# Three order strings of a one-core convolution-and-gate kernel are laid anew

## The chip, the core and the metric

The kernel runs on one core of a Trainium2 chip. The core has five instruction streams that run side by side: PE (TensorE, matrix products), DVE (VectorE), ACT (ScalarE), POOL (GpSimd) and SP (SyncE, which here only starts transfers). Each stream takes its instructions in the order of the program and waits, by semaphores, for what it needs from others. Matrix products land in PSUM; an *eviction* copies or casts a PSUM tile to SBUF, and is done by DVE or by ACT. Transfers between SBUF and DRAM are started from SP, ACT or POOL.

The metric is the device time of one execution in microseconds (us). Of the kernel before there are three timed runs and one profiled execution.

## The reference

For one sequence of 2048 positions and 512 channels the forward pass is

```python
xn = _layernorm(x)
# S4 part: a diagonal state space model with 128 modes a channel, as a long convolution
P = exp(dt * A * l)                       # l = 0 .. 2047
K = einsum("dn,dnl,dn->dl", C, P, dt * B).real
s = irfft(rfft(pad(xn)) * rfft(pad(K)))[:L] + xn * Dskip
# gate: two matrix products, 512 -> 1792 -> 512
g = silu(silu(xn @ w1) @ w2)
out = x + s * g
```

The kernel must give `out` and, for a given `grad_out`, the gradients of u, A (real, imaginary), B (real, imaginary), C (real, imaginary), log_dt, Dskip, w1 and w2: twelve outputs in bf16.

## The kernel before

The work is cut into stages. Stage 1 makes the powers of the modes, runs the gate's forward pass and stores most of its results in DRAM. Stage 2, the *table stage*, makes the filter K for four blocks of 128 channels. For a block b = 1 to 3 the kernel loads the compact tables X and XYc (`open_tables`, `open_y`), ACT copies XYc into CY (`copy_tables`, L869 and L870), and DVE multiplies the tables out in five steps (`chunk_tables`, L884 to L905: products over X, over CY, and three more over X). PE then makes K from X and CY (`chunk_K`, tile ps_k, evicted to Kout), and it also transposes the finished rows of X (`gen_xt`, L1012, tile pt_xt, evicted to XT and stored as XTd for the backward pass). Beside this the layernormed input xn and the gradient tile DS go through the first half of a Fourier transform (`spectrum`: tiles ps_f, evicted to FA; a *turn* of FA, that is two 32 x 32 block transposes on DVE at L162; ps_s, evicted to FX), and w2 is transposed (`gen_w2t`, tile pt_w, evicted to w2o). `store_K` (L956) writes K to Kud in DRAM.

Stage 3 reads K back in another layout (`load_K`, K_b, L976 to L983, started from SP, ACT and POOL), transforms it (FA, FX again), multiplies the spectra with those of xn and DS (XP loads on POOL, `cplx_mul` L125 and L126), transforms back (tile ps_i, evicted to FZ, turned at L162; then ps_v), and writes the convolution outputs DXC and S_s (`evs`, L104). Stage 5 runs the backward pass of the state space part (`Slabs.steps`: Gbd L1624, ps_V to Vb, T L1649), of the gate (`all_dh`, `all_dx`, ps_w to KXW, dhT L1740), the weight gradients (`grads`, L1901, from the tile dhc, which is loaded at L1870) and the output (`Out0`, L1450 to L1463: for each of eight pieces of the sequence, loads of zS, zg and zx from SP, two DVE products, and a store that is started one piece later; a piece has two buffers a name).

What sets the order of all this are strings written out by hand. `play` (L109) takes a string, and for each letter lets one generator go one step on; the letter names the generator (`t` one group of transposes, `g` one table step, `u` a step of the spectrum of xn, `f` that of DS, and so on). If the letter is a capital, the PSUM evictions of that step are done by DVE (`k.by_dve`, L77 in `ev`, L104 in `evs`), otherwise by ACT. All instructions are then in the order in which the steps ran, each on its engine. Steps that only start transfers (`o`, the loads of X; `k` in stage 3, those of XP) are letters too.

```python
def ev(k, out, in_):
    (k.nc.vector.tensor_copy if k.by_dve else k.nc.scalar.copy)(out=out, in_=in_)

    for ch in score:
        kk.by_dve = ch.isupper()
        next(parts[ch.lower()], None)
```

SCORE_1 orders stage 1, SCORE_2 the table stage, SCORE_3 the leftovers of the table stage, the filter transform and the convolutions, and SCORE_5 the backward pass in three parts. What a string does not reach is drained behind it.

Of the kernel before, what the change touches and what calls it, by code (L numbers as in the profile page):

```python
# [30 lines left out]

SCORE_1 = "pppppggppgppppppppgpggpppppppgppppgppgppgppppppppppgppppppppgppgpppgppppgpgpppppMgppppgppppppppgpppppgppmpgpmpppgpgppmpmpgpppgpgmppppgppmpMmgpgpmmpmggGmttgmtmGtgmtgggGgggGGg"
SCORE_2 = (
    "uguuuuuutUtuwKttttgTckggktukggttttotututuTtgtg",
    "tcutgutgkTkgkkoutt",
    "uutuutuuuuKgugwctUktuw",
    "uuwgtugkgttuTtktWuKkKkt",
)
SCORE_3 = (
    "TTtTUU",  # L40
    "FFFFffTuffTqfkqqqfffqFfkUffFffTfDfuTfUfDffkdkd",
    "FaddaafadkfdddFaknddFdafaffFbDsvvvavdsndngbFagnsbdbkgggadkadidaidadDpDbiabjpdsjbaaadxipbxvvxvxxvexsizjBgziepgegggzjtzxxtizeszjzXzibtzjbyybfebpbybsbpbxxjpssxxpyxlxxesxzglzczqxsjesysezzyzlsczYsCzsYZCsCCCC",
)
SCORE_5 = (
    "uywuuWWLWhywl",
    "yLhWYluYYyLwlwwLuhylwulHlllHwYllwYyYuhLwlyLlyWhwwyhwywLHwllYWwLWLlwHWylyWLlWhwwllyLoholoolhlLlYoLooYyllYlHllxlxxLlLhxlxlxxll",
    "zxzhxHHfxHxhfxhfhxxxxHxHxHxhhtftttfhxxxfHxzmxxHxtftttffzmtMtftxmxtxmtzfffMxfMftftmftxzMMxzffzmrtzrmzrr",
)


# [1903 lines left out]
```

## Time and profile before

| what | value |
|---|---|
| median of 3 runs | 688.61 us (688.0 to 692.97) |
| the profiled execution | 691.96 us, span 690.2 us |
| granted PE clock over the span | 0.943 of full speed |
| busy, share of the span: PE, DVE, ACT, POOL | 84%, 84%, 64%, 14% |
| DRAM read and written | 76.81 and 67.65 MB, 209 GB/s over the span |

The page gives one execution. Busy time is the time in which an engine runs an instruction, so a span of 690.2 us with PE at 84% has some 110 us in which PE waits for another engine, a transfer, or a buffer. Times of a trace's rows are counted from the start of the span. The table stage begins near 150.8 us; K is stored near 241.4 us; the convolutions end near 408 us.

### The profile page before, as it was taken

The page shows a single profiled execution, that of the slowest core. Times are in us where ns is not written, and L with a number is a line of the kernel's source. Part 1 is how long each engine was busy: PE and PEld are TensorE (multiplying, and loading weights), DVE is VectorE, ACT ScalarE, POOL GpSimd, SP SyncE. Part 2 cuts the span into 40 slices and gives each one's busy share as a digit, 9 for nine tenths or more (in the row PEclk, how much of TensorE's full clock was granted, in tenths as well). Part 3 has the DMA queues.
Part 4 walks back from the last instruction along what each step waited for, and adds up shares of the span by engine and source line. Part 5 has one row for each costly group of instructions (what it writes and reads, how often), then busy time and mean ns, then how long its engine had stood idle before and what let it go on. Part 6 is the DMA issues. An engine that isn't in the chain of part 4 may idle for free. (4 is left out here: it accounts for less than half of the span.)

```text
span 690.2 us, 14325 instructions
## 1 busy us (share of the span) xinstructions
PE 576.4 (84%) x5668; PEld 339.3 (49%) x5668; DVE 578.2 (84%) x954; ACT 444.3 (64%) x537; POOL 95.4 (14%) x170
## 2 busy tenths in 40 slices
PE   2977978877666868889988778899987989999896
PEld 1433433346545756566765544354544535454452
DVE  6898999789977467998999879977888978888656
ACT  4899999968779646999799615454164344443221
POOL 1120000201001232111232142121011000000000
PEclk9999999988988889999999989899998999999998
DMA  8664758778896699946477688979979559677786
GB/s 253 229 226 173 271 198 274 263 256 241 234 267 204 202 243 307 302 161 196 130 239 205 150 244 225 245 208 185 225 198 229 152 171 250 185 235 236 275 260 214
DMA packets 173622, 154.58 MB, mean 224 GB/s; under 512 B 70574, under 2 KB 141750, under 8 KB 173556
## 3 DMA queue, kind: packets, MB, share of 16 engines
q1 hardware_dynamic: 157428, 112.70, 57.3%
q0 software_dynamic: 11920, 38.08, 17.3%
q10 hardware_dynamic: 4208, 2.89, 1.5%
q8 instruction: 44, 0.72, 0.4%
q14 instruction: 22, 0.18, 0.1%
HBM read 76.81 MB, written 67.65 MB: 209 GB/s over the span
## 5 line engine op out<-in xcount | busy, mean ns | idle before, releaser
L723 PE MATMUL ps_h<-XNT,W 128*128 128x512 bf16 x224 | 58.2, 409 | 21.3 <-ACT hs L77 14.6
L1739 PE MATMUL ps_da<-DOT,W2T 128*128 128x512 bf16 x224 | 57.1, 401 | 0.7 <-DVE Vb L77 0.5
L696 PE MATMUL ps_o<-W,aT 128*128 128x512 bf16 x224 | 55.3, 396 | 1.4 <-ACT aT L725 1.4
L1801 PE MATMUL ps_dx<-KXW,dhT 128*128 128x512 bf16 x224 | 53.4, 386 | 0.0
L1568 PE MATMUL ps_w<-DO_all,KXW 128*128 128x512 bf16 x224 | 51.9, 379 | 0.7 <-DVE KXW L77 0.4
L1901 PE MATMUL ps_w<-dhc,xn 128*128 128x448 bf16 x256 | 49.7, 352 | 2.0 <-DVE o10b L77 1.9
L77 ACT CAST FA<-ps_f 128x1024 bf16<-128x1024 f32 x43 | 42.4, 1046 | 11.0 <-DMA K_b<-Kud 7.0
L77 ACT CAST FZ<-ps_i 128x1024 bf16<-128x1024 f32 x46 | 45.8, 1047 | 3.9 <-PE ps_i L187 3.8
L723 PEld LDWEIGHTS <-W 128*128 128x128 bf16 x224 | 22.7, 102 | 51.2 <-issue 26.7
L1810 ACT ACTIVATE dxn<-dxn,c,rstd 128x512 f32<-128x512 f32 x16 | 13.0, 814 | 47.4 <-DVE c L1809 47.4
L173 PE MATMUL ps_s<-FA,Wf 128*64 128x256 bf16 x384 | 35.0, 316 | 8.0 <-DVE FA L162 5.3
L1740 DVE TENSOR_TENSOR dhT<-ps_da,sd 128x1024 bf16<-128x1024 f32 x28 | 34.1, 1220 | 8.6 <-ACT sd L213 4.5
L696 PEld LDWEIGHTS <-aT 128*128 128x128 bf16 x224 | 22.9, 103 | 31.8 <-issue 6.5
L1901 PEld LDWEIGHTS <-xn 128*128 128x128 bf16 x256 | 25.0, 98 | 26.0 <-issue 2.5
L77 ACT CAST Vb<-ps_V 128x1024 bf16<-128x1024 f32 x22 | 22.0, 1014 | 24.5 <-PE ps_V L1637 18.2
L1739 PEld LDWEIGHTS <-W2T 128*128 128x128 bf16 x224 | 22.3, 103 | 28.9 <-issue 8.1
L187 PEld LDWEIGHTS <-Vi 64*128 64x128 bf16 x576 | 28.3, 98 | 15.6 <-issue 4.5
L1360 PE MATMUL ps_v<-FZ,TI 128*128 128x256 bf16 x192 | 26.4, 290 | 11.2 <-DVE FZ L162 10.3
L187 PE MATMUL ps_i<-XP,Vi 64*128 64x256 bf16 x256 | 32.0, 288 | 2.8 <-ACT KXW L77 2.4
L1801 PEld LDWEIGHTS <-dhT 128*128 128x128 bf16 x224 | 21.4, 99 | 24.6 <-issue 2.8
L725 ACT ACTIVATE aT<-ps_h 128x1024 bf16<-128x1024 f32 x28 | 31.2, 1115 | 3.3 <-PE ps_h L723 3.2
L1568 PEld LDWEIGHTS <-KXW 128*128 128x128 bf16 x224 | 20.8, 98 | 25.0 <-issue 3.3
(311 smaller groups left out, 1454.2 us busy)
## 6 DMA issues: line engine op xcount, KB each, us to landing
XTd<-XT SPq DMA_DIRECT2D x20, 512.0 KB
XP<-UXd POOLq DMA_DIRECT2D x16, 512.0 KB, 5.1
XTl<-XTd SPq DMA_DIRECT2D x31, 256.0 KB
hTd<-hs SPq DMA_DIRECT2D x28, 256.0 KB
aTd<-aT SPq DMA_DIRECT2D x28, 256.0 KB
dhc<-dhd SPq DMA_DIRECT2D x16, 448.0 KB
XYd<-XYg SPq DMA_DIRECT2D x25, 256.0 KB
hsb<-hTd SPq DMA_DIRECT2D x18, 256.0 KB
```

The costliest lines, as they stand in the source:

```text
L77: (k.nc.vector.tensor_copy if k.by_dve else k.nc.scalar.copy)(out=out, in_=in_)
L173: nc.tensor.matmul(out=ps[64 * h:64 * h + 64, c, j], lhsT=k.Wf[:, c, 0:64], rhs=A[:, 2 * (v + j) + h], start=True, stop=True)
L187: nc.tensor.matmul(out=ps[:, h, j], lhsT=Vc[z], rhs=y[z, c, v % 4 + j, :], start=(n == 0), stop=(n == len(Y) - 1))
L696: nc.tensor.matmul(out=pso[:], lhsT=aT[:, ft, tt * P:(tt + 1) * P], rhs=W2[:, ft, :], start=(ft == 0), stop=(ft == FT - 1))
L723: nc.tensor.matmul(out=ps[:, j], lhsT=W1[:, dk, ft * P:(ft + 1) * P], rhs=XNT[:, dk], start=(dk == 0), stop=(dk == DK - 1))
L725: nc.scalar.activation(out=aT[:, f0:f0 + 2, :], in_=ps[:], func=ACT.Silu)
L1360: k.nc.tensor.matmul(out=ps[:, j], lhsT=k.TI[:, t0 + j, c, :], rhs=Z[:, 2 * (t0 + j) + c], start=(c == 0), stop=(c == 1))
L1568: nc.tensor.matmul(out=ps[:], lhsT=A[:, t, :], rhs=k.DO[:, t, :], start=(t == 0), stop=(t == T - 1))
L1739: nc.tensor.matmul(out=ps[:, j], lhsT=self.W2T[:, ft // 2, dk, j * P:(j + 1) * P], rhs=self.DOT[tc_][:, dk], start=(dk == 0), stop=(dk == ...
L1740: nc.vector.tensor_tensor(out=self.dhT[:, f0:f0 + 2, :], in0=ps[:], in1=sd[:], op=ALU.mult)
L1801: nc.tensor.matmul(out=psx[:], lhsT=dhT[:, ft, t % 4 * P:(t % 4 + 1) * P], rhs=self.W1T[:, ft, :], start=(ft == 0), stop=(ft == FT - 1))
L1901: nc.tensor.matmul(out=ps[:], lhsT=k.xn[:, t, dk * P:(dk + 1) * P], rhs=ch[i][:, t, :], start=(t == 0), stop=(t == T - 1))
```

## The change

Only the three strings SCORE_2, SCORE_3 and SCORE_5 are written anew. SCORE_1, every function and the set of matrix products stay. The strings were laid with a planner in which transfers of different queues are taken to share the rate of the memory. Each step occurs as often as before; what changes is where it stands and which engine does its evictions. The first part of SCORE_2 and the last of SCORE_5:

```diff
 SCORE_2 = (
-    "uguuuuuutUtuwKttttgTckggktukggttttotututuTtgtg",
+    "uuuuugutTTUKtTWuKuTtkTtgcTgtkgggttuuuoguttutcTkT",
...
 SCORE_5 = (
...
-    "zxzhxHHfxHxhfxhfhxxxxHxHxHxhhtftttfhxxxfHxzmxxHxtftttffzmtMtftxmxtxmtzfffMxfMftftmftxzMMxzffzmrtzrmzrr",
+    "zxHxzhzHxHxhxhfHxfxfxxxHhfxxHhttHftthxxxhfxzmxHxfxttxfxmxfttxftMzxtttxmttffffMtMmtzMffzzffmrtfmrzmrzmr",
```

What it moves on the engines is seen in their instructions. On DVE, where the first table step of block 1 (L901 with 128x1792) begins in the table stage, the row before it is the last small step of block 0. The order before:

```order
L905 TENSOR_TENSOR X<-m_1686 128x2x128
L77 CAST FA<-ps_f 128x4x64x4
L162 STREAM_TRANSPOSE FA<-FA 128x32x2x32 x2
L901 TENSOR_TENSOR m_1879<-X 128x1792
L903 TENSOR_TENSOR m_1880<-X 128x7x128 x2
L904 TENSOR_TENSOR X<-m_1879 128x7x128
L905 TENSOR_TENSOR X<-m_1880 128x7x128
```

And the same place in the new order:

```order
L905 TENSOR_TENSOR X<-m_1710 128x2x128
L77 COPY XT<-pt_xt 128x1024 x2
L77 CAST FA<-ps_f 128x4x64x4
L77 COPY XT<-pt_xt 128x1024
L77 COPY w2o<-pt_w_1848 128x1024
L77 CAST Kout<-ps_k 128x41x16
L162 STREAM_TRANSPOSE FA<-FA 128x32x2x32 x2
L77 COPY XT<-pt_xt 128x1024 x2
L901 TENSOR_TENSOR m_2043<-X 128x1792
L903 TENSOR_TENSOR m_2044<-X 128x7x128 x2
```

Seven evictions that ACT did, or that DVE did later, now stand on DVE before the first step of block 1.

On DVE at the border of the convolutions and the backward pass, the last turn and the five last evictions of DXC, before:

```order
L162 STREAM_TRANSPOSE FZ<-FZ 128x32x2x32 x2
L104 TENSOR_SCALAR DXC<-ps_v 128x4x256 x5
L77 CAST KXW<-ps_w_5948 128x512
L1624 TENSOR_TENSOR Gbd<-Gt,MK 128x16x32 x2
L77 CAST Vb<-ps_V 128x4x256
L1624 TENSOR_TENSOR Gbd<-Gt,MK 128x16x32 x2
L77 CAST KXW<-ps_w_5970 128x512
L1718 COPY DOT<-pt_do 128x1024
```

And now:

```order
L77 CAST FZ<-ps_i 128x2x2x64x4
L162 STREAM_TRANSPOSE FZ<-FZ 128x32x2x32 x2
L104 TENSOR_SCALAR DXC<-ps_v 128x4x256 x5
L1624 TENSOR_TENSOR Gbd<-Gt,MK 128x16x32 x2
L77 CAST Vb<-ps_V 128x4x256
L1624 TENSOR_TENSOR Gbd<-Gt,MK 128x16x32 x2
L77 CAST KXW<-ps_w_5950 128x512
L1718 COPY DOT<-pt_do 128x1024
```

The first KXW cast, which stood ahead of Gbd, is gone from there, and the cast that is left stands behind the second Gbd.

On SP at the end of the program, where `Out0` stores a piece of the output (L91) and loads zS, zg and zx of the next (L1450), before:

```order
L1450 DMA zg<-gd 128x1024
L1450 DMA zx<-in_A_u_dram 128x1024
L1517 DMA out_dram<-ob_9034 128x4x128
L91 DMA out_dram<-zS 128x1024
L1450 DMA zS<-Sd 128x1024
L1450 DMA zg<-gd 128x1024
L1450 DMA zx<-in_A_u_dram 128x1024
L1787 DMA out_dram<-O_9022 128x512
L1787 DMA out_dram<-O_9079 128x512
L91 DMA out_dram<-zS 128x1024 x2
```

And now, from the loads of the last piece but one on:

```order
L1450 DMA zx<-in_A_u_dram 128x1024
L91 DMA out_dram<-zS 128x1024
L1450 DMA zS<-Sd 128x1024
L1450 DMA zg<-gd 128x1024
L1450 DMA zx<-in_A_u_dram 128x1024
L1517 DMA out_dram<-ob_8997 128x4x128
L1517 DMA out_dram<-ob_9003 128x4x128
L1787 DMA out_dram<-O_8840 128x512
L1787 DMA out_dram<-O_9035 128x512
L91 DMA out_dram<-zS 128x1024 x2
```

Between the last loads and the stores of the last two pieces there were two other output stores; now there are four. One step of `Out0` more stands near the start of the string's last part.

More of the change, by code (lines that the diff above doesn't have):

```diff
@@ L33 @@
 SCORE_2 = (
-    "uguuuuuutUtuwKttttgTckggktukggttttotututuTtgtg",
-    "tcutgutgkTkgkkoutt",
-    "uutuutuuuuKgugwctUktuw",
-    "uuwgtugkgttuTtktWuKkKkt",
+    "uuuuugutTTUKtTWuKuTtkTtgcTgtkgggttuuuoguttutcTkT",
+    "Tgt",
+    "TgktggkkotTguuuuuuuuwtuuuttUKkkWkttctwggugtuuutugtuWuTtTKkK",
+    "kT",
 )
 SCORE_3 = (
-    "TTtTUU",
-    "FFFFffTuffTqfkqqqfffqFfkUffFffTfDfuTfUfDffkdkd",
-    "FaddaafadkfdddFaknddFdafaffFbDsvvvavdsndngbFagnsbdbkgggadkadidaidadDpDbiabjpdsjbaaadxipbxvvxvxxvexsizjBgziepgegggzjtzxxtizeszjzXzibtzjbyybfebpbybsbpbxxjpssxxpyxlxxesxzglzczqxsjesysezzyzlsczYsCzsYZCsCCCC",
+    "TTu",
+    "FkFFFFFfqfutqqqftfffqTFkfFnfDfkUfffffTDfffddFuddU",
+    "aaafdkAffdddnaknDsdFadffafaFiDbbvBvvbvkddnsgksbadagasbgagFkdddGddaDqpijDbdpabaaadxxxiexvjepvtvvizzjgzBxjptgszxesgiggietxxzizizjzjbbbXfzyygbpsbbbeycbpxsyxzxxppsxsxxxelxcsjjzescszyselzsyzsyszlYzZZCCCCC",
 )
 SCORE_5 = (
-    "uywuuWWLWhywl",
-    "yLhWYluYYyLwlwwLuhylwulHlllHwYllwYyYuhLwlyLlyWhwwyhwywLHwllYWwLWLlwHWylyWLlWhwwllyLoholoolhlLlYoLooYyllYlHllxlxxLlLhxlxlxxll",
-    "zxzhxHHfxHxhfxhfhxxxxHxHxHxhhtftttfhxxxfHxzmxxHxtftttffzmtMtftxmxtxmtzfffMxfMftftmftxzMMxzffzmrtzrmzrr",
+    "uyuuwuuLlWWhywwWYuYYLwhllhwwllLlYHHWwlhLuyWll",
+    "LyhwWYLYwlHYlylWLllwwywwllywylWHllywlwYllYWyLHwwwylylloYHoLoYlhoLHoolollhlYLxlhLxLLxxxllxxll",
+    "zxHxzhzHxHxhxhfHxfxfxxxHhfxxHhttHftthxxxhfxzmxHxfxttxfxmxfttxftMzxtttxmttffffMtMmtzMffzzffmrtfmrzmrzmr",
 )
```

## The prediction

> **What bounds the kernel now.** I first read the table of windows, since the three order strings that change belong to stages that lie one behind the other. Columns: span of the window, busy time of PE, weight loads, VectorE (DVE), ScalarE (ACT) and GpSimd (POOL), granted clock, DMA share, GB/s.
>
> ```profile
> core 0: us, PE busy (x) PEld busy (x) DVE busy (x) ACT busy (x) POOL busy (x), PEclk, DMA share, GB/s
> 0.00:150.80 150.80, 117.45 (x571) 54.02 (x572) 130.87 (x320) 132.87 (x177) 16.98 (x33) 0.95 0.72 241
> 150.80:246.00 95.20, 69.14 (x1569) 55.27 (x1570) 75.34 (x127) 73.70 (x83) 12.37 (x22) 0.86 0.75 226
> 246.00:277.50 31.50, 22.83 (x257) 18.25 (x256) 21.04 (x27) 18.15 (x20) 10.16 (x19) 0.95 1.05 286
> 277.50:407.00 129.50, 109.44 (x1293) 80.33 (x1292) 121.20 (x108) 104.82 (x113) 32.70 (x54) 0.95 0.67 198
> 407.00:520.00 113.00, 103.73 (x954) 53.20 (x953) 97.27 (x143) 51.10 (x57) 18.69 (x34) 0.96 0.91 219
> 560.00:690.20 130.20, 121.04 (x682) 60.88 (x680) 96.45 (x177) 45.38 (x71) 0.56 (x1) 0.97 0.77 236
> ```
>
> The first window is laid by SCORE_1, which stays, so its 150.8 us stay. The table stage (to 246) is bound by no engine: PE, DVE and ACT are each busy 69 to 75 of 95.2 us, and wait for one another. In 246 to 277.5 the filter K comes back from DRAM, and the DMA share stands at its ceiling. From 277.5 to 407 DVE is busy 121.2 of 129.5, with ACT close behind. After 407 PE carries it: 103.7 of 113, then 121.0 of 130.2. So an order can win most in the table stage, where 95.2 − 75.3 = 19.9 us of DVE are idle, and little elsewhere.
>
> Next I read the waits and the DVE's own rows there, to see what the idle time is.
>
> ```profile
> DVE XT L77 <- PE pt_xt L1012: 16.0, 3, 9.7
> ACT FA L77 <- DMA K_b<-Kud: 7.0, 1, 7.0
> ACT Y L1035 <- DMA XYy<-XYd: 17.6, 1, 17.6
> ```
> ```profile
> 160.97 1.22 DVE L77 CAST FA<-ps_f 128x1024 bf16<-128x1024 f32 x1 [1.30 <-PE ps_f L148]
> 162.30 4.52 DVE L162 STREAM_TRANSPOSE FA<-FA 128x2048 f32<-128x2048 f32 x2
> 166.75 1.04 DVE L901 TENSOR_TENSOR m<-X 128x1792 bf16<-128x1792 bf16 x1
> ...
> 215.76 4.51 DVE L162 STREAM_TRANSPOSE FA<-FA 128x2048 f32<-128x2048 f32 x2 [4.17 <-ACT FA L77]
> ...
> 230.74 0.28 DVE L905 TENSOR_TENSOR X<-m 128x256 bf16<-128x256 bf16 x1
> ...
> 242.23 1.29 DVE L77 COPY XT<-pt_xt 128x1024 bf16<-128x1024 bf16 x2 [9.66 <-PE pt_xt L1012]
> 243.69 0.69 DVE L77 COPY XT<-pt_xt 128x1024 bf16<-128x1024 bf16 x1 [0.17 <-issue]
> 244.33 2.36 DVE L77 CAST FX<-ps_s 128x1024 bf16<-128x1024 f32 x2
> ```
> ```profile
> 241.39 2.34 SPq L956 DMA_DIRECT2D Kud<-Kout  x2
> ```
>
> The DVE multiplies the tables of three blocks one after the other, and the last product of block 3 ends at 230.74 + 0.28 = 231.0. Then the PE makes the last part of K, and at 241.39 SP stores it. **This chain, table products to K stored to K loaded, is the path of the table stage.** That ACT then waits 7.0 us for K_b says the same from the other end.
>
> **The change part by part.** No instruction is added or removed. Twelve PSUM evictions go from ACT to DVE over all stages behind SCORE_1 (in net), and each engine's order is new. Prices by these groups (columns: count, busy us, mean ns, idle before):
>
> ```profile
> L77 DVE COPY XT<-pt_xt 128x1024 bf16<-128x1024 bf16 x10 | 6.8, 686 | 16.2 <-PE pt_xt L1012 16.0 <-issue 0.2
> L77 DVE CAST FA<-ps_f 128x1024 bf16<-128x1024 f32 x5 | 5.8, 1215 | 1.3 <-PE ps_f L148 1.3
> L77 ACT COPY XT<-pt_xt 128x1024 bf16<-128x1024 bf16 x30 | 30.1, 1051 | 2.7 <-PE pt_xt L1012 1.1 <-DMA X<-XYd 0.8 <-ACT Kout L77 0.7
> L77 ACT CAST FA<-ps_f 128x1024 bf16<-128x1024 f32 x28 | 27.3, 1056 | 9.6 <-DMA K_b<-Kud 7.0 <-PE ps_f L148 2.5
> L77 ACT CAST Kout<-ps_k 128x656 bf16<-128x656 f32 x8 | 5.7, 712 | 8.9 <-PE ps_k L938 8.9
> ```
>
> *Term 1, the table chain.* Before, between the FA cast and the first product of block 1 the DVE has only a turn. Now seven evictions stand there beside the cast: five XT copies, one w2o copy and one Kout cast. Back to back an XT copy takes 1.29 / 2 = 0.65, so 5 × 0.65 = 3.3; w2o is as large, 0.7; the Kout cast is not in the trace on DVE and lies between ACT's 0.71 and the 1.22 of the larger cast; I take 0.8, being nearer in size to the first. Sum 4.8. These copies must also wait for their transposes. Such a wait costs between 0 and the mean 16.0 / 3 = 5.3 of the row above; I take 3, because the transposes follow each other closely in the order. So block 1 begins some 8 us later. One thing gives back: before, the turn at 215.76 stood 4.17 us for ACT's casts, and a DVE that comes later finds them done, so about 8 − 4 = 4 us are left at the end of block 3. Of this a further half microsecond goes as some K work of earlier blocks is now further ahead. **+3.5 at the store of K**; its ends are −10.1 (second rival) and +18.5 (first rival).
>
> *Term 2, behind the table chain up to 407.* Between K's store and the filter transform the order leaves out two FX casts (2.36) and one XT copy (0.65) on DVE: −3.0. Up to the last turn of that transform DVE then takes over about three casts (six FA in a row instead of four are two of them), 3 × 1.22 = +3.6; those can fall into the 31.5 − 21.0 = 10.5 us that DVE idles in 246 to 277.5. In the convolutions one cast goes back to ACT in net, −1.1 where DVE is busy 121.2 of 129.5. The ends are −3.0 − 1.1 = −4.1 and −3.0 + 3.6 − 1.1 = −0.5. As DVE waits there for K's loads and not for itself, I take a value nearer to the second, **−1.8**.
>
> [...]
>
> *Term 3, the start of the backward pass.* Before, DVE comes out of the five last convolution evictions and stands 2.10 us for a KXW cast whose matmuls have just begun; behind it wait the two products Gbd that need nothing of it.
>
> ```profile
> 406.03 2.35 DVE L104 TENSOR_SCALAR DXC<-ps_v 128x1024 bf16<-128x1024 f32 x2 [0.48 <-PE ps_v L1360]
> 410.48 0.69 DVE L77 CAST KXW<-ps_w 128x512 bf16<-128x512 f32 x1 [2.10 <-PE ps_w L1568]
> 411.09 1.28 DVE L1624 TENSOR_TENSOR Gbd<-Gt,MK 128x512 bf16<-128x512 bf16 x2
> ```
>
> Now Gbd stands first, and what it feeds (ps_V, then Vb) starts as much earlier: **−2.0** of the 2.10; it is 0 if the Gt loads are the next to be late. ACT's 17.6 us for XYy stay; ACT has little to do at that point in either order.
>
> *Term 4, the tail.*
>
> ```profile
> 663.40 0.86 SPq L91 DMA_DIRECT2D out_dram<-zS  x1
> 668.78 0.32 SPq L1450 DMA_DIRECT2D zS<-Sd  x1
> ...
> 680.78 0.33 SPq L1450 DMA_DIRECT2D zS<-Sd  x1
> ...
> 684.74 0.69 DVE L1462 TENSOR_TENSOR zS<-zS,zg 128x1024 bf16<-128x1024 bf16 x1 [2.85 <-DMA zg<-gd]
> ...
> 687.97 0.29 SPq L1084 DMA_DIRECT2D out_dram<-row  x1
> ```
> ```profile
> 664.69 18.32 PE L1901 MATMUL ps_w<-dhc,xn 128*128 128x448 bf16 x96
> ```
>
> The last PE work of size ends at 664.69 + 18.32 = 683.0, the last output row leaves at 687.97. What lies between is SP's chain of Out0: store a piece, wait until it landed, load the next into its buffer, multiply, and so on, (680.78 − 668.78) / 2 = 6.0 us a round. DVE's last reduction for the row stands behind the last such product and its 2.85 us of waiting. In the new order one more of these pieces is done before the tail, and the x steps end earlier, so that the PE has nothing but its last groups. The wait goes, and PE's end is next: an o10b eviction and its store. **−2.5** (0 to −4: the row can't leave before PE's last group, 683.0 and its eviction).
>
> *Sum:* 3.5 − 1.8 − 2.0 − 2.5 = −2.8. The profiled execution took 691.96 (span 690.2), so it becomes 689.2. The median of the three runs is 688.61, 3.35 below the profiled one; on that footing 688.61 − 2.8 = **685.8**. Terms 1 and 4 have the widest ends.
>
> **The rivals.**
>
> *First, slower: the PE is held behind the transposes.* PE, like DVE, takes its instructions in order. If a group of transposes that now stands early waits for the whole table of its block, PE holds everything behind it, spectra and chunks alike, for the delay of each block: 8 + 7 + 3.5 = +18.5 at the store of K (block 2 being late by 8 less the 0.5 to 1.1 us it waited for X). The decision lies where the first of those groups reads its X rows: from the third product on, the rows of a group are the last to be ready. For it speaks that DVE has already waited 9.66 us in one piece for transposes. Against it: before, transposes of block 1 ran at 173.95, while the table's last products ran at 183.76, so a group needs only its rows.
>
> ```profile
> 173.95 1.63 PE L1012 MATMUL pt_xt<-ident_bfloat,X 128*128 128x128 bf16 x26
> ...
> 183.76 0.28 DVE L905 TENSOR_TENSOR X<-m 128x256 bf16<-128x256 bf16 x1
> ```
>
> Time: 688.61 + 18.5 − 1.8 − 2.0 − 2.5 = 700.8.
>
> *Second, faster: ACT paces the table stage.* ACT loses there seven XT copies (7 × 1.05), two w2o (2 × 1.02, their size being XT's) and a Kout cast (0.71): 10.1 us. If it was ACT's evictions that made PE wait for PSUM, the stage shortens by up to that: 688.61 − 10.1 − 1.8 − 2.0 − 2.5 = 672.2. For it: DVE copies XT in 686 ns and ACT in 1051, and the first of the waits on DVE (4.17) is for ACT. Against it: ACT itself idles 21.5 of the 95.2 us. [...]
>
> *Third, it does nothing.* The change is laid for transfers that share the rate. If loads were in time already (ACT's wait for K_b apart, no wait above is for a load that the order moves by much), the table chain's 3.5 and the gains behind it both fall into idle time: 688.6.
>
> **How the numbers follow.** Forecast 0.42, first rival 0.25, second 0.22, third 0.11. This kernel's measurement tells 1% from no change, that is 681.7 and 695.5. The forecast's own range, from its terms' ends without the rivals (3 us either way for the wait in term 1, −0.5 to −4.1, 0 to −2.1, 0 to −4), runs from about 679 to 695 (−6.9 and +8.8 about 685.8); a sixth of it, 0.07, lies under 681.7 and with later stages gone wrong 0.07 above 695.5. Faster: 0.22 + 0.07 = 0.29. Slower: 0.25 + 0.07 = 0.32. Same: the rest, 0.39. Range: 673 to 701. It takes in the time of the first rival and stops just above that of the second, 672.2, which is ACT's whole 10.1 us and so the far end of that case.
>
> **What would show it.** Term 1: the first L901 product of block 1 near 175 instead of 166.75, the last of block 3 near 235, the store of Kud near 245. Term 2: the first forward cast of K_b and its turn 0 to 2 us after their old places relative to the store of Kud. Term 3: no DVE gap of 2 us before the first Gbd. Term 4: no DVE wait for zg at the end, and the last PE group within 5 us of the end. The prediction is wrong if the table stage ends more than 5 us away from 246 + 3.5 on either side, if the stage after 277.5 shows a new stall of the DVE over 5 us (a load of XP behind others), or if PE in the last window stands for dhc loads that now go out later.

## The result, and the profile after

The changed kernel takes 684.72 us (median of 7 runs, 681.39 to 685.46), and the kernel before, run again beside it, 692.46 us (median of 7, 688.0 to 694.85). The ratio is **0.989, with a 95% interval of 0.986 to 0.993**: some 7.5 us less. The forecast was 685.8 us and a gain of 2.8 us. That the absolute time is met so well owes something to chance, since the first three runs of the kernel before, from which the forecast started, lay low (688.61); the gain itself is more than twice the forecast.

The profiled execution took 685.07 us (span 683.0). Its windows behind the first, four of them cut as before and the last one at the end of the span:

```profile
core 0: us, PE busy (x) PEld busy (x) DVE busy (x) ACT busy (x) POOL busy (x), PEclk, DMA share, GB/s
150.80:246.00 95.20, 66.81 (x1549) 54.89 (x1546) 81.13 (x137) 63.55 (x72) 12.47 (x23) 0.87 0.76 229
246.00:277.50 31.50, 22.72 (x264) 18.23 (x262) 23.27 (x33) 17.52 (x19) 10.48 (x20) 0.95 1.00 264
277.50:407.00 129.50, 108.64 (x1319) 81.18 (x1317) 124.32 (x107) 105.40 (x113) 32.35 (x53) 0.97 0.71 207
407.00:520.00 113.00, 102.62 (x1011) 54.45 (x1012) 100.33 (x150) 52.54 (x59) 20.11 (x36) 0.98 0.91 220
560.00:683.00 123.00, 113.91 (x650) 57.31 (x647) 91.98 (x169) 42.93 (x69) 0.00 (x0) 0.98 0.77 235
```

In the table stage ACT's busy time falls from 73.7 to 63.6 us and DVE's rises from 75.3 to 81.1; ten evictions have changed sides there. The windows have fixed borders, so a stage that ends earlier shows in them only through the one behind it. The rows of single instructions say more. DVE's rows at the first tables of block 1:

```profile
160.55 1.29 DVE L77 COPY XT<-pt_xt 128x1024 bf16<-128x1024 bf16 x2
161.76 1.22 DVE L77 CAST FA<-ps_f 128x1024 bf16<-128x1024 f32 x1
163.69 0.69 DVE L77 COPY XT<-pt_xt 128x1024 bf16<-128x1024 bf16 x1 [0.72 <-PE pt_xt L1012]
165.00 0.69 DVE L77 COPY w2o<-pt_w 128x1024 bf16<-128x1024 bf16 x1 [0.61 <-PE pt_w L1070]
166.70 0.84 DVE L77 CAST Kout<-ps_k 128x656 bf16<-128x656 f32 x1 [1.02 <-PE ps_k L938]
167.46 4.50 DVE L162 STREAM_TRANSPOSE FA<-FA 128x2048 f32<-128x2048 f32 x2
171.88 1.25 DVE L77 COPY XT<-pt_xt 128x1024 bf16<-128x1024 bf16 x2
173.05 1.07 DVE L901 TENSOR_TENSOR m<-X 128x1792 bf16<-128x1792 bf16 x1
```

The seven evictions are there. The Kout cast took 0.84 us on DVE, where 0.8 was estimated, and the three waits for PE are 0.72 + 0.61 + 1.02 = 2.35 us. The first product starts at 173.05 instead of 166.75. SP's rows around the store of K in the new order:

```profile
244.87 2.06 SPq L956 DMA_DIRECT2D Kud<-Kout  x2
...
251.80 0.65 SPq L976 DMA_DIRECT2D K_b<-Kud  x1
```

K is stored at 244.87, 3.5 us later than in the profile of before, but the first load of K_b goes out 6.9 us behind the store; before it was 251.32 − 241.39 = 9.9, by ACT's row here (the same view of the kernel before):

```profile
251.32 0.35 ACTq L977 DMA_DIRECT2D K_b<-Kud  x1
```

Whether these differences belong to the change can't be said from two profiles. The table below shows why.

### The profile page after: what moved, and what is told of

Its sections match the earlier page's. It is cut to its first block, busy times and chain, and to the rows that moved or that the text cites. A ratio compares the mean times of both kernels' runs of the same rounds, so it can differ in the third digit from the quotient of the medians.

```text
span 683.0 us, 14339 instructions
## 1 busy us (share of the span) xinstructions
PE 565.2 (83%) x5668; PEld 336.6 (49%) x5668; DVE 586.6 (86%) x967; ACT 430.9 (63%) x524; POOL 95.4 (14%) x170
## 5 line engine op out<-in xcount | busy, mean ns | idle before, releaser
L723 PE MATMUL ps_h<-XNT,W 128*128 128x512 bf16 x224 | 59.9, 419 | 21.7 <-ACT hs L77 14.9
L1739 PE MATMUL ps_da<-DOT,W2T 128*128 128x512 bf16 x224 | 54.6, 388 | 1.2 <-ACT Vb L77 1.2
L696 PE MATMUL ps_o<-W,aT 128*128 128x512 bf16 x224 | 52.4, 382 | 1.4 <-ACT aT L725 1.4
L1901 PE MATMUL ps_w<-dhc,xn 128*128 128x448 bf16 x256 | 49.1, 353 | 0.0
L77 ACT CAST FZ<-ps_i 128x1024 bf16<-128x1024 f32 x44 | 43.0, 1037 | 5.3 <-PE ps_i L187 5.0
L77 ACT CAST FA<-ps_f 128x1024 bf16<-128x1024 f32 x39 | 37.9, 1054 | 9.2 <-PE ps_f L148 9.0
L1901 PEld LDWEIGHTS <-xn 128*128 128x128 bf16 x256 | 25.0, 98 | 23.7
L187 PEld LDWEIGHTS <-Vi 64*128 64x128 bf16 x576 | 27.7, 94 | 14.0 <-issue 4.2
L77 ACT CAST FX<-ps_s 128x1024 bf16<-128x1024 f32 x28 | 27.6, 1031 | 10.5 <-PE ps_s L173 5.1
L173 PEld LDWEIGHTS <-Wf 128*64 128x64 bf16 x384 | 23.5, 118 | 19.9 <-issue 15.8
```

The costliest lines, as they stand in the source:

```text
L173: nc.tensor.matmul(out=ps[64 * h:64 * h + 64, c, j], lhsT=k.Wf[:, c, 0:64], rhs=A[:, 2 * (v + j) + h], start=True, stop=True)
L187: nc.tensor.matmul(out=ps[:, h, j], lhsT=Vc[z], rhs=y[z, c, v % 4 + j, :], start=(n == 0), stop=(n == len(Y) - 1))
L696: nc.tensor.matmul(out=pso[:], lhsT=aT[:, ft, tt * P:(tt + 1) * P], rhs=W2[:, ft, :], start=(ft == 0), stop=(ft == FT - 1))
L723: nc.tensor.matmul(out=ps[:, j], lhsT=W1[:, dk, ft * P:(ft + 1) * P], rhs=XNT[:, dk], start=(dk == 0), stop=(dk == DK - 1))
L1739: nc.tensor.matmul(out=ps[:, j], lhsT=self.W2T[:, ft // 2, dk, j * P:(j + 1) * P], rhs=self.DOT[tc_][:, dk], start=(dk == 0), stop=(dk == ...
L1901: nc.tensor.matmul(out=ps[:], lhsT=k.xn[:, t, dk * P:(dk + 1) * P], rhs=ch[i][:, t, :], start=(t == 0), stop=(t == T - 1))
```

## The experiments

Each is an edit of one of the two kernels that leaves no work out. With them there are twelve profiles beside the two; each string is old in some of them and new in others, so that each stretch can be read several times with the same code. These are the stretches (us), from the times of single rows: *store*, the start of K's store; *load*, from there to the first load of K_b; *turn 2*, from the store to the end of the second turn of FA; *conv*, from there to the last turn of FZ; *Gbd*, from there to the first Gbd; *T*, from there to the end of the last T product; *grads*, from there to PE's last L1901 matmul; *end*, from there to the end of the span.

| kernel | ratio to before | store at | load | turn 2 | conv | Gbd | T | grads | end |
|---|---|---|---|---|---|---|---|---|---|
| before | 1 | 241.4 | 9.9 | 41.8 | 117.4 | 10.4 | 148.7 | 123.2 | 7.2 |
| changed | 0.989 | 244.9 | 6.9 | 39.8 | 115.1 | 6.8 | 145.9 | 123.7 | 6.9 |
| fwd_new | 0.995 | 241.1 | 7.0 | 42.3 | 115.0 | 9.3 | 147.9 | 122.9 | 8.1 |
| bwd_new | 0.991 | 243.8 | 9.4 | 42.2 | 116.0 | 7.2 | 145.5 | 123.2 | 7.1 |
| bwd_early | 0.994 | 242.9 | 9.6 | 41.9 | 117.8 | 7.3 | 146.0 | 123.2 | 8.5 |
| bwd_late | 0.999 | 242.6 | 9.8 | 42.2 | 117.0 | 9.2 | 147.8 | 123.0 | 7.7 |
| table_new | 0.999 | 241.3 | 7.1 | 40.5 | 117.4 | 10.5 | 148.8 | 121.9 | 7.6 |
| conv_new | 0.996 | 241.6 | 9.6 | 42.0 | 115.5 | 10.3 | 148.7 | 123.0 | 7.8 |
| extra_store | 0.989 | 241.8 | 8.9 | 40.4 | 114.6 | 6.9 | 146.0 | 123.1 | 8.5 |
| no_caps | 0.985 | 240.9 | 7.1 | 39.1 | 114.4 | 7.1 | 146.2 | 122.4 | 7.4 |
| l_first | 1.002 | 242.7 | 9.7 | 42.3 | 117.3 | 7.7 | 151.9 | 122.1 | 9.0 |
| head_new | 1.006 | 242.7 | 9.5 | 42.3 | 116.0 | 7.3 | 154.6 | 122.3 | 7.9 |
| z3 | 0.980 | 243.0 | 7.0 | 39.1 | 115.0 | 7.1 | 145.6 | 122.5 | 3.3 |
| before_z3 | 0.989 | 242.1 | 9.2 | 41.8 | 116.7 | 10.1 | 148.6 | 120.9 | 3.3 |

Read down a column, *load*, *conv*, *Gbd* and *T* fall into groups by the string they belong to (apart from l_first and head_new, whose strings are mixed, and from extra_store's *load*). *Turn 2* does so with one exception: fwd_new, with the new strings, has 42.3, as the old ones have. The column of the store does not: with the old SCORE_2 it lies between 241.4 and 243.8, with the new one between 241.1 and 244.9 (the letters of no_caps apart).

**Which string brings it.** Four kernels, each with some of the new strings:

```diff
  fwd_new:    SCORE_2 and SCORE_3 new, SCORE_5 old
  bwd_new:    SCORE_2 and SCORE_3 old, SCORE_5 new
  bwd_early:  only SCORE_5[0] and SCORE_5[1] new
  bwd_late:   only SCORE_5[2] new
```

> SCORE_2 and SCORE_3 new, SCORE_5 as before. Theory A (the backward strings bring most of the gain): the profile puts the end of the convolutions 2 us earlier, so the ratio to the kernel before is about 0.997 (-2 us), and the last products of the state space part (T on DVE) end 1 to 3 us earlier than before, not 7. Theory B (the forward strings bring it): about 0.990 (-7 us). The store of K should come about 3.5 us later than before under both.

> SCORE_2 and SCORE_3 as before, SCORE_5 new. Theory A: 0.992 to 0.994 (-4 to -5.5 us), and everything up to 407 us as before. Theory B: 0.998 to 1.001.

> Only the first two parts of SCORE_5 new, its last part as before. Theory A: the gain of the backward strings arises here, 0.993 to 0.995 (-3.5 to -5 us), and the tail hands it on whole. Theory C (the tail is bound by the chain of output pieces on SP, which the last part of the string moves): 0.998 to 1.001, since the tail would take the gain back.

> Only the last part of SCORE_5 new. Theory A: 0.998 to 1.002, since DVE still waits for zg at the end of the changed kernel. Theory C, and the fourth term of the prediction: 0.995 to 0.997 (-2.5 us).

Measured: fwd_new 0.9948 (0.992 to 0.998), bwd_new 0.9913 (0.988 to 0.995), bwd_early 0.9935 (0.991 to 0.996), bwd_late 0.9988 (0.997 to 1.001). So the backward strings bring some 6 us and the forward ones 3.6 (together 9.6, more than the 7.5 of the whole, but within the intervals); theory A holds, theory B and C fall. The tail (bwd_late) gives 0.8 us, with an interval that takes in nothing and 2.3. Three readings of the profiles missed: K's store in fwd_new came at 241.08 and not 3.5 us late; the last T product of fwd_new ended 4.1 us earlier than before, not 1 to 3; and in bwd_new, whose code up to 407 us is as before, the store came 2.4 us later than before.

**What the forward strings do.**

```diff
  table_new:  SCORE_2 and SCORE_3[0] new, all else old
  conv_new:   SCORE_3[1] and SCORE_3[2] new, all else old
```

> SCORE_2 and the first part of SCORE_3 new, the rest as before. From the store of K to the first load of K_b 7.0 us, as in the changed kernel, against 9.9 before (the store shares the transfer engines with one 512 KB store of UXd less). Theory P (what the load gains, DVE's own work takes back before the second turn of the filter transform, which is reached no earlier): ratio 0.998 to 1.002. Theory Q (the load of K sets the path to the end): 0.995 to 0.996 (-3 us).

> SCORE_2 and the first part of SCORE_3 as before, the two later parts of SCORE_3 new. From the store of K to the first load of K_b about 10 us, as before. Theory P: the gain of the forward strings comes from the convolutions, 0.994 to 0.997 (-2 to -4 us), the last turn of FZ 2 us earlier relative to the second turn of the filter transform. Theory Q: 0.998 to 1.002.

Measured: table_new 0.9993 (0.997 to 1.001), conv_new 0.996 (0.994 to 0.998). The order of the table stage alone is worth nothing that can be measured, though it has the load at 7.1; the convolutions bring some 2.8 us. Both ratios are those of theory P. Its reason, that DVE's own work takes the load's gain back before the second turn, is not borne out: table_new reaches that turn after 40.5 us, the old order after 42.1 in the mean, and DVE is busy for only 27.7 of the 40.5. Where the rest of the gain goes is open; a gain of 2 us lies within table_new's interval.

What the convolutions gain can be read. The stretch *conv* in the kernel before and in the changed one, columns as in the windows above:

```profile
283.23:400.64 117.41, 99.55 (x1212) 73.38 (x1212) 110.98 (x102) 99.28 (x106) 27.48 (x45) 0.97 0.65 190
```
```profile
284.64:399.70 115.06, 96.61 (x1212) 73.13 (x1212) 110.99 (x97) 98.72 (x105) 28.32 (x47) 0.98 0.69 199
```

DVE is busy for the same 111.0 us and idle for 6.4 before and 4.1 now. In the means of the eight profiles with the old part and the six with the new one it is idle for 6.0 and 4.0 us, which is the whole difference of the stretch: DVE stands less.

Why K_b's load goes out sooner: in the kernel before, POOL starts a store of UXd (512 KB) in the same moment as SP and ACT store K. POOL's rows of the kernel before, and then of the changed kernel:

```profile
241.14 0.22 POOL L946 TENSOR_TENSOR Kout<-Kout,DskT 128x16 bf16<-128x16 bf16 x1 [4.36 <-ACT Kout L77]
241.36 0.56 POOL L1103 DMA_DIRECT2D UXd<-FX  x1
241.91 0.55 POOL L91 DMA_DIRECT2D W2Td<-w2o  x1
```
```profile
244.63 0.21 POOL L946 TENSOR_TENSOR Kout<-Kout,DskT 128x16 bf16<-128x16 bf16 x1 [5.84 <-ACT Kout L77]
244.84 0.56 POOL L91 DMA_DIRECT2D W2Td<-w2o  x1
```

To test it, such a transfer was put back:

```diff
 def store_K(k):
+    k.nc.gpsimd.dma_start(k.idle_d[:], k.xn[:, 0:4, :])   # 512 KB to a scratch tensor
```

> The changed kernel with one more transfer: POOL stores 512 KB of xn to a scratch tensor in DRAM just ahead of the store of K; nothing reads it. If transfers that share the engines are why K_b is loaded 3 us earlier after K's store, the 7.0 us go back to 9.5 to 11, and the first turn of the filter transform comes about 3 us later. The whole time: 0.989 to 0.991 of the kernel before if that lies beside other work (theory P), 0.993 to 0.995 if the load is on the path (theory Q). If the store only waits for its own issue and receipt, the 7.0 us stay.

```profile
241.78 2.55 SPq L957 DMA_DIRECT2D Kud<-Kout  x2
244.43 5.15 SPq L91 DMA_DIRECT2D XTd<-XT  x2
250.67 0.65 SPq L977 DMA_DIRECT2D K_b<-Kud  x1
```

In SP's rows the load now goes out 250.67 − 241.78 = 8.9 us behind the store. That is 1.9 of the 2.6 us that the column "load" shows between the orders; it is less than the 9.5 that was expected, so by this one profile the UXd store is most of the cause but need not be all of it. The first turn came 14.6 us behind the store, against 13.2 in the changed kernel: 1.4 us later and not 3. The whole time stayed at 0.9892 (0.987 to 0.992), as in the changed kernel. The 0.993 to 0.995 of theory Q lies outside this interval, and table_new with its early load gains nothing that shows, so a load of K that is 2 to 3 us earlier or later hardly moves the end.

**DVE's copies in the table stage.**

```diff
-    "uuuuugutTTUKtTWuKuTtkTtgcTgtkgggttuuuoguttutcTkT",
+    "uuuuugutttUkttwukuttkttgctgtkgggttuuuoguttutctkt",
```

> The changed kernel with every T, W and K of the first part of SCORE_2 in small letters: the seven evictions ahead of block 1's tables and the others of that part go back to ACT, in the new order. The first term of the prediction (VectorE's copies delay the table chain, +3.5 at the store of K) gives a store of K 3 us earlier than in the profiles with the capitals (241.1 to 244.9), and a ratio of 0.984 to 0.987. The second rival (ACT paces the stage) gives a store 3 us or more later and 0.993 or more. Theory N (the stage has slack on both engines there): the store within 2 us of 242.4 and 0.988 to 0.991.

Measured: 0.9853 (0.983 to 0.988), the store at 240.9. DVE's rows at block 1:

```profile
159.96 1.23 DVE L77 CAST FA<-ps_f 128x1024 bf16<-128x1024 f32 x1 [0.77 <-PE ps_f L148]
165.56 4.50 DVE L162 STREAM_TRANSPOSE FA<-FA 128x2048 f32<-128x2048 f32 x2 [4.38 <-ACT FA L77]
169.99 1.05 DVE L901 TENSOR_TENSOR m<-X 128x1792 bf16<-128x1792 bf16 x1
```

The time is in the range of the first term, though its interval and that of the changed kernel overlap (0.983 to 0.988, 0.986 to 0.993), so that the copies cost something is likely, not shown. Against the mean of the five profiles with the capitals (242.4) the store is 1.5 us earlier, from one profile; that is half of what the first term gave, and within theory N's 2 us. The rows show how the price is paid back: without the copies DVE stands 4.38 us for ACT ahead of the same turn, and block 1 starts only 2 us earlier than the mean of 172.0 (170.9 to 173.1). The second rival, ACT as the pace, falls: ACT has ten evictions more here, and nothing is later.

**The border to the backward pass.** One letter is moved in the kernel before:

```diff
-    "uywuuWWLWhywl",
+    "uywuuLWWWhywl",
```

> The kernel before with one letter moved: in the first part of SCORE_5 the first L stands ahead of the two W, so Gbd, Vb and the second Gbd stand ahead of both KXW casts on DVE, as in the changed kernel. The third term of the prediction: from the last turn of FZ to the first Gbd 7 us instead of 10.4, the last T product 2 us earlier, ratio 0.997. If the KXW casts only move behind Gbd and cost there what they cost before: first Gbd earlier by 3 us, but the last T product where it was, 0.999 to 1.001.

DVE's rows there:

```profile
409.85 1.28 DVE L1624 TENSOR_TENSOR Gbd<-Gt,MK 128x512 bf16<-128x512 bf16 x2
411.64 1.23 DVE L77 CAST Vb<-ps_V 128x1024 bf16<-128x1024 f32 x1 [0.51 <-PE ps_V L1637]
412.78 1.28 DVE L1624 TENSOR_TENSOR Gbd<-Gt,MK 128x512 bf16<-128x512 bf16 x2
413.98 0.68 DVE L77 CAST KXW<-ps_w 128x512 bf16<-128x512 f32 x1
416.91 0.69 DVE L77 CAST KXW<-ps_w 128x512 bf16<-128x512 f32 x1 [2.25 <-PE ps_w L1568]
```

Measured: 1.0024 (1.000 to 1.005). Counted from the last turn of FZ, Gbd and the first Vb behind it come some 2.8 us earlier, but the wait of 2.10 us for the KXW matmuls is now one of 2.25 us behind them. From the last turn of FZ to the last T product the kernel takes 7.7 + 151.9 = 159.6 us, before 10.4 + 148.7 = 159.1. Nothing is won by this alone.

**Where the backward order wins.** In PE's waits, from 404 to 565 us, one row differs much. First the kernel before, then the changed one (the columns are us in all, times, the longest); in l_first it reads as in the kernel before:

```profile
PE ps_S L1667 <- DVE T L1649: 10.2, 5, 2.8
```
```profile
PE ps_S L1667 <- DVE T L1649: 4.7, 2, 3.3
```

A kernel with the first 45 letters of the new order ahead of the rest of the old one was to show where that happens:

> The kernel before with the first 45 letters of the new backward order, and behind them the letters that are left in the old order. From the first Gbd to the last T product it was 148.7 us before and is 145.5 to 146.0 with all of the new strings, and PE's waits for the T products fall from 10.2 to 4.7 us. If they fall in this head: about 146 and a ratio of 0.992 to 0.995. If in the later letters: 148 to 149 and 0.996 to 0.998 (the border of the stages alone). Worse than before, over 1.000, if the old rest doesn't fit the new head.

Measured: 1.0061 (1.004 to 1.008), and from FZ to the last T product 7.3 + 154.6 = 161.9 us. The wait for T is 8.7 us in five pieces. This is the last of the three cases: the old rest doesn't fit the new head.

So neither the border nor the head wins by itself; the whole of the two strings does (152.7 to 153.3 us in the six profiles that have them, against 157.1 to 159.3 in the six that have the old ones unchanged). Which of its pairs of letters brings PE's T products sooner was not found.

The wait for T falls by 5.5 us, as much as the stretch is shorter in the mean, but it is not the account of the gain. From the last turn of FZ to the last T product, the windows of the kernel before, of fwd_new (the old backward strings too) and of the changed kernel are:

```profile
400.64:559.81 159.17, 142.65 (x1335) 74.86 (x1336) 137.79 (x202) 69.34 (x76) 26.84 (x48) 0.94 0.84 206
```
```profile
398.45:555.66 157.21, 138.64 (x1315) 74.02 (x1336) 137.63 (x203) 69.37 (x76) 26.21 (x47) 0.96 0.81 207
```
```profile
399.70:552.39 152.69, 136.50 (x1335) 72.61 (x1336) 138.43 (x205) 66.62 (x74) 26.16 (x47) 0.98 0.88 214
```

All have the same 1336 weight loads, so PE has the same work in them. In the means of the twelve profiles counted above, PE's idle time falls only from 18.0 to 16.9 us, since other waits grow as the one for T shrinks (in the changed kernel 1.9 us for dhT and 1.9 for XTl, which the kernel before has not). What falls is PE's busy time, from 140.4 to 136.1 us, with a granted clock of 0.97 to 0.98 in the six profiles with the new strings and of 0.94 to 0.96 in the other six. Of those six, the two at 0.96 have the two shortest stretches (157.1 and 157.2 us). So the larger part of the 5.5 us is the same matmuls done in less time at a higher granted clock. Whether the new order brings the higher clock about, by the way in which it spreads PE's waits, is shown by no run; the wait for T and the clock were not separated.

**The tail.** Of the pieces of the output each has two buffers, so the load of a piece stands on SP until the store of the piece before the last has landed. With three it need not:

```diff
-            t = self.pool.tile([P, TS, D], BF16, name=nm, tag=nm, bufs=2)
+            t = self.pool.tile([P, TS, D], BF16, name=nm, tag=nm, bufs=3)
```

z3 is the changed kernel with this line, before_z3 the kernel before with it.

> The changed kernel with three buffers instead of two for the pieces of the output (zS, zg, zx), so that the load of a piece does not wait until the store of the piece before the last has landed. If the chain store, landing, load, product sets the end (what stopped the fourth term of the prediction), SP's waits of 4 to 6 us ahead of these loads go, DVE's wait for zg at the end goes, and the ratio is 0.984 to 0.986 (3 us less than the changed kernel); the last row then leaves within 4 us of PE's last group. If not, 0.988 to 0.990 as the changed kernel.

> The kernel before with three buffers instead of two for the pieces of the output. If the chain of the pieces on SP sets the end in the old order too: from PE's last weight gradient group to the end 3.3 us instead of 7.2, and a ratio of 0.993 to 0.995. If the old order hides it: 0.998 to 1.001.

The end of the changed kernel, on SP, DVE and PE, and then that of z3, on SP, PE and ACT:

```profile
653.98 0.34 SPq L91 DMA_DIRECT2D out_dram<-zS  x1
660.54 0.32 SPq L1450 DMA_DIRECT2D zS<-Sd  x1
...
661.91 0.38 SPq L91 DMA_DIRECT2D out_dram<-zS  x1
666.22 0.32 SPq L1450 DMA_DIRECT2D zS<-Sd  x1
...
680.83 0.29 SPq L1084 DMA_DIRECT2D out_dram<-row  x1
```
```profile
664.55 0.69 DVE L1462 TENSOR_TENSOR zS<-zS,zg 128x1024 bf16<-128x1024 bf16 x1 [8.91 <-DMA zg<-gd]
670.15 0.69 DVE L1462 TENSOR_TENSOR zS<-zS,zg 128x1024 bf16<-128x1024 bf16 x1 [3.80 <-DMA zg<-gd]
```
```profile
649.66 26.46 PE L1901 MATMUL ps_w<-dhc,xn 128*128 128x448 bf16 x139
```
```profile
646.82 0.34 SPq L91 DMA_DIRECT2D out_dram<-zS  x1
648.40 0.32 SPq L1450 DMA_DIRECT2D zS<-Sd  x1
...
672.77 0.29 SPq L1084 DMA_DIRECT2D out_dram<-row  x1
```
```profile
654.72 17.57 PE L1901 MATMUL ps_w<-dhc,xn 128*128 128x448 bf16 x92
```
```profile
672.32 0.53 ACT L77 CAST o10b<-ps_w 128x448 bf16<-128x448 f32 x1 [2.49 <-PE ps_w L1901]
```

In the changed kernel SP stands 6.2 us (653.98 + 0.34 to 660.54) and then 3.9 us between a store and the next load. SP's waits for the landing of earlier stores, from 560 us to the end, are these in the changed kernel and in z3:

```profile
SPq L1450 <- DMA out_dram<-zS: 22.7, 6, 5.4
```
```profile
SPq L1450 <- DMA out_dram<-zS: 1.6, 1, 1.6
```

In the changed kernel DVE waits 8.91 and 3.80 us for zg, and the last products of f and the row, queued behind on DVE, are late; PE's last group ends at 676.1, the row leaves at 680.83. In z3 the gap on SP is 1.2 us, the last row goes out 0.5 us behind PE's last group (672.29), and the end follows in 3.3 us: an eviction and its store.

Measured: **z3 0.980 (0.977 to 0.983), 677.75 us**, more than was expected (0.984 to 0.986), and before_z3 0.989 (0.986 to 0.992), also more (0.993 to 0.995). Of before_z3's gain the profile shows 3.9 us in the end and 2.3 in the stretch of the weight gradients, where PE stood 1.9 us for one eviction of DVE (o10b) before and doesn't now; the other profiles with two buffers have 121.9 to 123.7 in that stretch, so the 2.3 are read from one pair. z3 beats both kernels. The kernel no_caps with three buffers was not run.

## Why the prediction was right or wrong

The sign and the range were right, but the range, 673 to 701, is wide. Of its three classes the largest chance, 0.39, stood on a change of less than 1%; the ratio says 1.1% (0.7 to 1.4), at the border to "faster" with its 0.29. The size was short: terms 1 and 4 came to nothing, term 2 to twice its size, and the stretch of term 3 gained more than the term, by something that the prediction did not have. That 684.72 lies so near to the 685.8 is luck: the kernel before took 692.46 us when it ran again and not 688.61. None of the prediction's three signs of being wrong appeared. Means are over all profiles of the table with the same string.

*Term 1, the table chain, +3.5.* The mechanism is there: the copies stand ahead of block 1, their own time is the 4.8 us that was estimated, and the waits were 2.35 us in one profile instead of 3. What failed is that the two were added up as a delay. Block 1 starts 5.1 us later (172.0 against 166.9 in the mean of eight profiles of the old order), where 8 was forecast, and without the copies DVE stands 4.38 us for ACT at that place (no_caps, where block 1 starts at 170.0), so that they themselves make up only 2 of the 5.1. What is given back was right: the last product of block 3 ends 0.7 us late in the mean (232.6 against 231.9), so 4.4 us are made good where 4 were expected, and 0.8 more up to K's store, which comes 0.1 us early (242.4 against 242.5), where half a microsecond was expected. The term is 0 and not +3.5. That the first profile showed 244.87 and so hit the forecast to 0.1 us was luck: the same code gave 241.1 to 244.9. The copies may cost something, as the time of no_caps suggests; if so, the rest of the new order of this stage pays it.

*Term 2, to the end of the convolutions, −1.8.* It is about −3.9: −1.9 from the store to the second turn (40.2 against 42.1 in the mean, single profiles 39.1 to 42.3) and −2.0 in the convolutions (114.9 against 117.0). That is within the term's ends, but the value was taken too near to the small one. In the convolutions it is not one cast fewer on DVE, as the prediction had it, for DVE is busy as long as before; it stands 2.0 us less. That DVE's FX casts left the store's neighbourhood was read rightly from the order, but what they took with them was overlooked: the 512 KB store that their last cast starts on POOL. With one such store put back beside K's, the first load of K_b goes out 8.9 us behind K's store and not 7.0 (extra_store), 1.9 us later. Between the two orders the load comes 2.6 us sooner behind the store, and at the second turn the new order is 1.9 us ahead.

*Term 3, −2.0.* The first Gbd is 2.9 us nearer to the turn in the mean, and what it feeds does start earlier: in l_first Vb comes 2.8 us sooner. The step that failed is the one that isn't written down, that this start is handed on to the end. With this letter alone the wait goes behind Gbd and Vb and is 2.25 us there, and nothing is gained (l_first, 1.002). The backward pass nevertheless gains 5.5 us (152.9 against 158.4, l_first and head_new left out), which the prediction had nowhere: it put no term on the rest of these two strings, since it took PE's busy time behind 407 us (103.7 of 113) as given, so that an order could win little there. What they bring is, by the windows, some 4.3 us of PE's busy time at a higher granted clock and some 1.2 us of its idle time; why the clock is higher stays open.

*Term 4, −2.5.* It was read as a chain, correctly, and judged broken, wrongly. The new order still takes its stores and loads of pieces one behind the other at the end, as the rows of SP show: DVE waits 12.7 us for zg in both kernels. The end stayed at 7 to 8.5 us behind PE's last group, and bwd_late gives 0.999. One piece more at the start does not help if the last ones still run back to back; a third buffer does (z3, 3.3 us to the end).

*Sum.* 0 − 3.9 − 5.5 − 0 = −9.4, which the interval of the ratio (0.986 to 0.993, −9.8 to −5.1 us) takes in. Of the rivals, the first falls: PE was not held behind the transposes, for K's store is not later in the mean, and DVE's longest wait for them is 8.54 us, where it was 9.66. The second falls with no_caps: ACT does not pace the table stage. The low granted clock of the table stage does not go with the most idle time of PE: by the prediction's own rows PE idles 33.4 us in the first window, at a clock of 0.95, and 26.1 in the table stage, at 0.86; the window behind has the same share of idle time, some 27%, and 0.95. After the change PE idles 28.4 us in the table stage, and its clock is 0.87. The third, that it does nothing, falls by the interval.

## What to carry to other kernels

Ask of an order what stands beside a store that others wait for, in the transfers of all queues, and not only what engine work stands there (one 512 KB store beside K's put the load of K 1.9 us later in extra_store, and left the whole time at 0.989); and of a wait that seems to go, where the instruction that waited is put (in l_first 2.10 us ahead of Gbd became 2.25 behind it). Where two buffers make a load wait for a store's landing at the end of a program, a third one was worth as much here as the whole new order of work (0.989 each alone, 0.980 together), and it left the order alone. And a wait that shrinks by as much as a stretch is not yet its cause: add up all of the engine's idle time in the stretch, and compare its busy time for the same work. A stage's boundary read from two profiles can be off by more than the term in question: here the same instructions reached the store of K between 241.4 and 243.8 us.

## What the runs showed of the hardware that was not expected

One 512 KB store that starts with the store of K (4 stores of 164 KB from two queues) delayed the first load that waits for K's store by 1.9 us in the one profile that tests it (8.9 us behind that store, against 7.0). In the backward stretch PE was busy for 138.6 to 142.7 us in profiles with a granted clock of 0.94 to 0.96, and for 135.7 to 136.5 us at 0.97 to 0.98, with the same 1336 weight loads. And the time at which identical code is at a given row varies by 2 to 4 us between profiles of one program, while stretches such as the convolutions (114.4 to 115.5 in six profiles) vary by one.
